# The smallest experts' tiles of a routed layer: 64 rows with high and low parts side by side, two products in place of three

## The chip, the cores and the metric

One core of a Trainium2 chip. The metric is the time of one execution on the device in microseconds; the kernel before takes 1523.02 us in the median of three runs.

## What is computed

Three parts, one behind the other (cut to what matters here):

```python
x = attention(q, k, v, proj)           # 2 x 8 heads, 768 tokens, 64 wide; tokens see only keys of their own bucket
x = sinkhorn_moe(x)                    # 8 experts, every token through every expert
def moe2(x, w_skip, w_gate, w1, w2):   # the second layer: 1536 tokens x 512
    do_compute = x @ w_skip > 0
    e_idx = argmax(x @ w_gate, axis=1)             # one expert for each token kept
    for e in range(8):
        h = maximum(x[e_idx == e] @ w1[e], 0)      # 512 -> 1024
        y = gate * (h @ w2[e])                     # 1024 -> 512
    out = x; out[do_compute] += y
```

With the reference's inputs 815 tokens are kept; ordered by their counts in the first 768 tokens, the experts hold 204, 197, 161, 119, 82, 33, 12 and 7 of them.

## The kernel before

Attention, the first layer and the second layer run one behind the other; the change is in the second. There each expert has a slot of 128 or 256 rows. `order()` ranks the experts by their count in the first half of the tokens, and `SLOT` says which slot each rank gets: ranks 0, 1, 2 get slots 0, 2, 4, which hold two tiles of 128 rows, the others slots with one tile. `route` and `scat` write each token's row into a table in memory; tokens that find no room in their slot are worked off by a reserve loop at the end (`tc.If(n > 0)`), whose number of tiles `extras()` counts.

`TILES = [[0, 8], [1], [2, 9], [3], [4, 10], [5], [6], [7]]` gives the tiles of each slot, in the order of work. For a tile, `gather` fetches its 128 rows by an indirect DMA on GpSimd's queue; `xpose` transposes them on PE (`turn`, L912), ScalarE copies the bank as the high part (fp32r, L914) and VectorE subtracts it to get the low part (L915). `up` multiplies with the first weights (L935), ScalarE applies Relu (L944), `hpose` turns the result in two halves (again `turn`), `down` multiplies with the second weights (L954); VectorE scales and adds the input (`y`, L960), and GpSimd's queue scatters the rows to `out`.

Each f32 product is three fp32r products: high x high, high x low, low x high, with moving operands of 512 columns. The weights come as 1 MB loads on SP's queue; `split` makes one set of 128 x 512, high part on ScalarE (L487), low part on VectorE (L488). A set is asked for by `bget`, which first sees to it that the eight sets behind it have been put into the queues. There are 16 sets for an expert, 8 in `up` and 8 in `down`.

The order of the work is that of the program text. Each step s runs `up` of slot s and then `down` of slot s-1; the turns and transposes of neighbours hang into `up` as jobs, one after each set of weights from the second on:

```python
for s in range(NE):
    jobs = posing([t for t in TILES[s - 1] if t]) if s > 0 else []
    if s + 1 < NE:
        jobs += [lambda t=t: xpose(t) for t in TILES[s + 1]]
    up([t for t in TILES[s] if t], bget, jobs)
    if s > 0:
        down(TILES[s - 1], bget, posing(TILES[s]) if s == NE - 1 else ())
```

So a `down` of a single tile and the `up` of the next single tile stand side by side, and that `up` has up to six jobs. Turns and the banks of `down` share the PSUM pool `mpa` with four banks, which are handed out in turn; a bank is free when ScalarE and VectorE have read it. All queues are in order.

In attention, the set-up of the later layers is strewn among the units of work (`next(m)`): small tables on GpSimd (`bi`, `trip`, `padt`) and their casts on VectorE (`brow`, `tokb`). `padt` has its own place in the pool `kp`. In attention GpSimd makes the low parts of the probabilities (`Pq`, L269) and of v (`r` L230, `vt` L232).

Of the kernel before, what the change touches and what calls it, by code (L numbers as in the profile page):

```python
# [7 lines left out]
F32 = mybir.dt.float32  # L8
R = mybir.dt.float32r
F16 = mybir.dt.float16  # L10
BF = mybir.dt.bfloat16
I32 = mybir.dt.int32
AF = mybir.ActivationFunctionType
ALU = mybir.AluOpType
# [4 lines left out]
NE = 8  # L19
NTOK = 1536  # L20
# [4 lines left out]
TILES = [[0, 8], [1], [2, 9], [3], [4, 10], [5], [6], [7]]  # L25
NST = 11

SLOT = (0, 2, 4, 1, 3, 5, 6, 7)

CLOSE = 0  # L30
PADID = 4000
# [369 lines left out]
def moes(nc, tc, ctx, ident, big, xT, P, g):  # L401
    out = g["out"]
    dram = ctx.enter_context(tc.tile_pool(name="dr", bufs=1, space=DRAM))
    kp = ctx.enter_context(tc.tile_pool(name="kp", bufs=1))
    sp = ctx.enter_context(tc.tile_pool(name="sp", bufs=1))
# [9 lines left out]
    def PS():  # L415
        ring.append(ring.pop(0))
        return P[ring[-1]].tile([128, 512], F32, tag="s", name="mp")
# [189 lines left out]
        nc.vector.tensor_copy(out=tokb[:, :, a].rearrange("p (b j) -> p b j", b=2), in_=ti[:, a])  # L607
    nslot = NE * CAP + 128
    table = dram.tile([nslot, 3], I32, name="table")
    padt = kp.tile([128, nslot // 128, 3], I32, name="padt")  # L610
    nc.gpsimd.memset(padt, 0)
    nc.gpsimd.memset(padt[:, :, 1], int(PADID))
    nc.sync.dma_start(out=table.rearrange("(p j) c -> p j c", p=128), in_=padt)
# [89 lines left out]
    scap = kp.tile([128, 8], F32, name="scap")  # L703
    for r, sl_ in enumerate(SLOT):
        nc.gpsimd.memset(scap[:, r:r + 1], float(sl_ * CAP))
    sbase = kp.tile([128, 8], F32, name="sbase")
    dbl = kp.tile([128, 8], F32, name="dbl")
    perm = kp.tile([128, 8], I32, name="perm")

    def order():  # L710

        ps = PS()
        for j in range(6):
            nc.tensor.matmul(ps[:, 0:8], lhsT=onesb, rhs=rt[0, j][1], start=j == 0, stop=j == 5)
        w = sp.tile([128, 3, 8], F32, tag="ow", name="ow", bufs=1)
        q3 = sp.tile([128, 8, 8], F32, tag="oq", name="oq", bufs=1)
        s3 = [128, 8, 8]

        def row(t):
            return t.unsqueeze(1).to_broadcast(s3)  # L720

        def col(t):
            return t.unsqueeze(2).to_broadcast(s3)
        nc.vector.scalar_tensor_tensor(out=w[:, 0], in0=ps[:, 0:8], scalar=8.0, in1=eid, op0=ALU.mult, op1=ALU.subtract)
        nc.vector.tensor_tensor(out=q3, in0=row(w[:, 0]), in1=col(w[:, 0]), op=ALU.is_gt)
        nc.vector.tensor_reduce(out=w[:, 1], in_=q3, axis=AX.X, op=ALU.add)
        nc.vector.tensor_tensor(out=q3, in0=row(eid), in1=col(w[:, 1]), op=ALU.is_equal)
        nc.vector.tensor_tensor(out=q3, in0=q3, in1=row(scap), op=ALU.mult)
        nc.vector.tensor_reduce(out=sbase, in_=q3, axis=AX.X, op=ALU.add)
        nc.vector.tensor_scalar(out=dbl, in0=w[:, 1], scalar1=float(len(DOUBLE)) - 0.5, scalar2=128.0, op0=ALU.is_lt, op1=ALU.mult)  # L730
        nc.vector.tensor_copy(out=ebb, in_=sbase[0:1, :])
        nc.vector.tensor_tensor(out=q3, in0=row(sbase), in1=col(ebase), op=ALU.is_equal)
        nc.vector.tensor_tensor(out=q3, in0=q3, in1=row(eid), op=ALU.mult)
        nc.vector.tensor_reduce(out=w[:, 2], in_=q3, axis=AX.X, op=ALU.add)
        nc.vector.tensor_copy(out=perm, in_=w[:, 2])
# [149 lines left out]
    xgs = {}  # L885
    gt = {}
    hh = {}
    ht = {}
    hf = {}
    dn = {}  # L890

    def bank(name):
        return P[name].tile([128, 512], F32, tag="s", name="mp")

    def rows_of(t):
        return first[:, 0] if t == 0 else ids[:, t]

    def gather(t, at=None):
        if t == 0:
            xg = P["rx"].tile([128, 512], F32, tag="y", name="xg", bufs=2)  # L900
        else:
            xg = P["m2"].tile([128, 512], F32, tag="xg", name="xg", bufs=8)
        nc.gpsimd.indirect_dma_start(out=xg, out_offset=None, in_=out,
                                     in_offset=bass.IndirectOffsetOnAxis(ap=rows_of(t)[:, 0:1] if at is None else at, axis=0),
                                     bounds_check=NTOK - 1, oob_is_err=False)
        xgs[t] = xg

    def turn(src, tag, bufs):

        ps = bank("mpa")  # L910
        for c in range(4):
            nc.tensor.transpose(ps[:, 128 * c:128 * c + 128], src[c], ident)  # L912
        o = P["xo" if tag == "x3" else "m2"].tile([128, 2, 512], R, tag=tag, name=tag, bufs=bufs)
        nc.scalar.copy(out=o[:, 0, :], in_=ps)  # L914
        nc.vector.tensor_tensor(out=o[:, 1, :], in0=ps, in1=o[:, 0, :].bitcast(F32), op=ALU.subtract)  # L915
        return o

    def xpose(t):
        v = xgs[t].rearrange("p (q a) -> p a q", a=4)
        gt[t] = turn([v[:, c, :] for c in range(4)], *(("xt", 3) if t else ("x3", 1)))  # L920

    def hpose(t, q):
        v = hh[t].rearrange("p (q a) -> p a q", a=8)
        ht.setdefault(t, []).append(turn([v[:, 4 * q + c, :] for c in range(4)], "hT", 4))

    def up(tiles, nget, jobs=()):
        jobs = list(jobs)
        for t in tiles:
            hf[t] = [bank("mpb"), bank("mpb")]
        for k in range(8):  # L930
            w = nget()
            c, h_ = divmod(k, 2)
            for t in tiles:
                for n, (a, i_) in enumerate(((0, 0), (0, 1), (1, 0))):
                    nc.tensor.matmul(hf[t][h_], lhsT=gt[t][:, a, 128 * c:128 * c + 128], rhs=w[:, i_, :],  # L935
                                     start=c == 0 and n == 0, stop=c == 3 and n == 2)
            if k > 0 and jobs:
                jobs.pop(0)()
        for f in jobs:
            f()  # L940
        for t in tiles:
            hh[t] = P["m2"].tile([128, 1024], F32, tag="hf", name="hf", bufs=2)
            for h_ in range(2):
                nc.scalar.activation(out=hh[t][:, 512 * h_:512 * h_ + 512], in_=hf[t][h_], func=AF.Relu)  # L944

    def down(tiles, nget, jobs=()):
        jobs = list(jobs)
        for t in tiles:
            dn[t] = bank("mpa")
        for c in range(8):  # L950
            w = nget()
            for t in tiles:
                for n, (a, i_) in enumerate(((0, 0), (0, 1), (1, 0))):
                    nc.tensor.matmul(dn[t], lhsT=ht[t][c // 4][:, a, 128 * (c % 4):128 * (c % 4) + 128], rhs=w[:, i_, :],  # L954
                                     start=c == 0 and n == 0, stop=c == 7 and n == 2)
            if c > 2 and jobs:
                jobs.pop(0)()
        for t in tiles:
            y = P["rx"].tile([128, 512], F32, tag="y", name="y", bufs=2)
            nc.vector.scalar_tensor_tensor(out=y, in0=dn[t], scalar=rows_of(t)[:, 2:3].bitcast(F32), in1=xgs[t], op0=ALU.mult, op1=ALU.add)  # L960
            nc.gpsimd.indirect_dma_start(out=out, out_offset=bass.IndirectOffsetOnAxis(ap=rows_of(t)[:, 1:2], axis=0),
                                         in_=y, in_offset=None, bounds_check=NTOK - 1, oob_is_err=False)


    XB = {}
# [60 lines left out]
    for b in range(2):  # L1026
        accs[b] = big.tile([128, 6, 512], F32, tag="big", name="acc")
        acc = accs[b]
        for e in range(NE):
            last = b == 1 and e == NE - 1  # L1030
            hs = []
            for fc in range(4):
                w = W1.pop(fc)
# [20 lines left out]
                p = prod(0, 0)  # L1054
# [15 lines left out]
                p = prod(5, 6)  # L1070
# [13 lines left out]
                p = prod(2, 3)  # L1084
# [3 lines left out]
                for h_, c_ in ((h0, ca), (h1, cb)):  # L1088
                    nc.vector.scalar_tensor_tensor(out=h_[:, 1, :], in0=c_.rearrange("p a t -> p (a t)"), scalar=0.0,  # L1089
                                                   in1=h_[:, 0, :].bitcast(F32), op0=ALU.max, op1=ALU.subtract)  # L1090
# [4 lines left out]
            if last:  # L1095
# [6 lines left out]
                for t in range(6):  # L1102
                    y = PS()
                    for i in range(8):
# [5 lines left out]
                        n = 8 * (t - 4) + i  # L1110
# [20 lines left out]
                        for n, (a, i_) in enumerate(((0, 0), (0, 1), (1, 0))):  # L1131
                            nc.tensor.matmul(y, lhsT=hs[i][:, a, 128 * t:128 * t + 128], rhs=W2[i][:, i_, :],  # L1132
                                             start=i == 0 and n == 0, stop=i == 7 and n == 2)
                    nc.vector.scalar_tensor_tensor(out=acc[:, t, :], in0=y, scalar=Pm[:, 6 + t, e:e + 1], in1=acc[:, t, :],
                                                   op0=ALU.mult, op1=ALU.add)
# [16 lines left out]
            for i in range(8):  # L1152
                hook()
                w = W2.pop(i)
                h = hs[i]
                for t in range(6):
                    for n, (a, i_) in enumerate(((0, 0), (0, 1), (1, 0))):
                        nc.tensor.matmul(ys[t], lhsT=h[:, a, 128 * t:128 * t + 128], rhs=w[:, i_, :],  # L1158
                                         start=i == 0 and n == 0, stop=i == 7 and n == 2)
# [9 lines left out]
            for t in range(6):  # L1169
                y = ys[t]  # L1170
                p = Pm[:, 6 * b + t, e:e + 1]
# [25 lines left out]
    nc.vector.tensor_tensor(out=ab, in0=listp[:, 0:2], in1=ab, op=ALU.add)  # L1197
    nc.vector.scalar_tensor_tensor(out=second, in0=ab[:, 0:1], scalar=16.0, in1=ab[:, 1:2], op0=ALU.mult, op1=ALU.add)
    gather(8, second)
    load_rest()  # L1200
    hpose(0, 1)
    tg = [t for tiles in TILES for t in tiles if t not in (0, 8)]
    for t in tg[:7]:
        gather(t)
    tg = tg[7:]
    xpose(8)

    def posing(tiles):
# [18 lines left out]
    n = nc.values_load(xidx["n"][0:1, 0:1], min_val=0, max_val=NXT)  # L1227
    with tc.If(n > 0):
        for x in range(NXT):
            t = NST + x  # L1230
# [3 lines left out]
            def nget():  # L1234
                kind, h_, i = own.pop(0)
                if i == 0:
                    cur["r"] = load_raw(kind, t, h_, "raw")
                return split(cur["r"][:, 512 * i:512 * i + 512], nc.vector)
# [54 lines left out]
```

## Time and profile before

| | |
|---|---|
| median of 3 runs | 1523.02 us (1520.9 to 1524.86) |
| profiled execution | 1523.56 us, span 1521.7 us |
| PE busy | 1415.9 us, 93% |
| PE weight loads busy | 1240.7 us, 82% |
| VectorE busy | 899.5 us, 59% |
| ScalarE busy | 653.8 us, 43% |
| GpSimd busy | 895.9 us, 59% |
| chain that ended last | PE 59%, DVE 19%, POOL 15%, issue 3% |

The second layer lies between about 1364 and 1521.7 us. Shares over the whole span say little about it: its stages are read one by one below. In the rows, PE is TensorE's products and PEld its weight loads, DVE is VectorE, ACT ScalarE, POOL GpSimd. An instruction's time in a row reaches to its end, while the next may start before: VectorE's instructions on 128 x 512 show about 0.68 us each and follow each other every 0.60 us.

### The profile page before, as it was taken

How to read it: one execution, taken by the hardware profiler on the slowest of the kernel's cores; microseconds unless marked ns; L12 is line 12 of the kernel's file. 1: busy time of each engine (PE TensorE's matmuls, PEld its weight loads, DVE VectorE, ACT ScalarE, POOL GpSimd, SP SyncE). 2: the span in 40 equal slices, each digit the busy share in tenths (PEclk: the TensorE clock that was granted, in tenths of full speed). 3: DMA queues.
4: the chain of work that ended last, by engine and by line, in shares of the span. 5: the costliest groups of instructions: out<-in, count | busy, mean ns of one | idle time of the engine just before them, and what ended most of it. 6: DMA issues, size and time to landing. Idle time of an engine off the chain costs nothing.

```text
span 1521.7 us, 21039 instructions
## 1 busy us (share of the span) xinstructions
PE 1415.9 (93%) x7747; PEld 1240.7 (82%) x7747; DVE 899.5 (59%) x1778; ACT 653.8 (43%) x1015; POOL 895.9 (59%) x763
## 2 busy tenths in 40 slices
PE   6788777799999999999999999999999999998997
PEld 5677666578889889899898888989899898876886
DVE  7899989977625336254264736426244262555876
ACT  4777767742423333233333433333133232325665
POOL 3666666764665767657677656856667565512111
PEclk7999999999999999999999999999999999999999
DMA  5999999902121121211211412121211212527762
GB/s 148 192 207 202 203 200 183 171 30 82 57 83 56 56 83 57 83 56 56 84 56 56 164 58 56 56 83 56 83 56 56 84 56 84 194 67 241 258 249 69
DMA packets 224224, 166.27 MB, mean 109 GB/s; under 512 B 160023, under 2 KB 199063, under 8 KB 219761
## 3 DMA queue, kind: packets, MB, share of 16 engines
q1 hardware_dynamic: 219520, 154.69, 38.2%
q10 hardware_dynamic: 2448, 5.58, 1.7%
q0 software_dynamic: 2144, 4.57, 0.9%
q8 instruction: 63, 1.03, 0.3%
q14 instruction: 49, 0.39, 0.1%
HBM read 113.04 MB, written 7.77 MB: 79 GB/s over the span
## 4 chain that ended last, share of the span: by engine, by line
PE 59%; DVE 19%; POOL 15%; issue 3%; ACT 2%; DMA 1%; ACTq 0%; POOLq 0%; DVEq 0%
PE mp L1158 30%; PE mp L1041 15%; POOL w L473 8%; DVE m L252 5%; PE mp L935 4%; PE mp L954 4%; DVE m L254 3%; PE mp L1132 2%; DVE X L298 2%; POOL w L488 2%; POOL T L465 1%; DVE r L296 1%; POOL T L464 1%; DVE t L184 1%; PE mp L912 1%
## 5 line engine op out<-in xcount | busy, mean ns | idle before, releaser
L1158 PE MATMUL mp<-w,h 128*128 128x512 f32 x2160 | 501.5, 393 | 0.0
L1041 PE MATMUL mp<-x,w 128*128 128x384 f32 x2688 | 479.9, 337 | 14.5 <-POOL w L473 9.3
L1041 PEld LDWEIGHTS mp<-x,w 128*128 128x128 f32 x2688 | 467.2, 188 | 22.9 <-POOL w L473 14.1
L1158 PEld LDWEIGHTS mp<-w,h 128*128 128x128 f32 x2160 | 404.5, 188 | 85.8
L488 POOL TENSOR_TENSOR w<-raw,w 128x512 fp32r<-128x512 f32 x127 | 177.4, 1397 | 235.3 <-ACT w L487 235.3
L487 ACT CAST w<-raw 128x512 fp32r<-128x512 f32 x256 | 151.2, 620 | 193.3 <-PE mp L1158 175.1
L1175 DVE SCALAR_TENSOR_TENSOR acc<-mp,Pm,acc 128x512 f32<-128x512 f32 x78 | 54.1, 749 | 291.9 <-PE mp L1158 291.9
L269 POOL TENSOR_TENSOR Pq<-P,Pq 128x768 f16<-128x768 f32 x96 | 158.2, 1653 | 94.7 <-ACT Pq L266 87.0
L473 POOL TENSOR_TENSOR w<-raw,w 128x512 fp32r<-128x512 f32 x124 | 128.9, 1060 | 95.5 <-ACT w L469 95.5
L1085 ACT ACTIVATE h<-ca 128x768 fp32r<-128x768 f32 x64 | 54.3, 848 | 235.4 <-DVE ca L1049 235.4
L473 POOL TENSOR_TENSOR w<-T,w 128x1024 fp32r<-128x1024 f32 x62 | 149.7, 2415 | 0.0
L471 ACT CAST w<-T 128x1024 fp32r<-128x1024 f32 x64 | 67.3, 1052 | 174.2 <-POOL T L466 170.4
L243 PE MATMUL s<-k,t 128*128 128x384 f32 x264 | 70.4, 393 | 37.0 <-ACT P L261 31.7
L284 PE MATMUL b<-vt,T 128*128 128x193 bf16 x576 | 98.8, 261 | 2.5 <-DMA T<-Pq 2.5
L1049 DVE TENSOR_TENSOR u<-mp,p 128x384 f32<-128x384 f32 x64 | 35.6, 556 | 103.2 <-ACT p L1056 61.0
L285 PE MATMUL b<-vt,T 128*128 128x129 bf16 x576 | 95.1, 229 | 0.0
L488 DVE TENSOR_TENSOR w<-raw,w 128x512 fp32r<-128x512 f32 x129 | 84.3, 696 | 12.7 <-ACT w L487 12.5
L261 ACT ACTIVATE P<-s,m 128x768 f32<-128x768 f32 x66 | 65.4, 991 | 55.0 <-DVE m L254 35.1
L243 PEld LDWEIGHTS s<-k,t 128*128 128x128 f32 x264 | 48.7, 211 | 46.4 <-ACT P L261 38.8
L266 ACT CAST Pq<-P 128x768 f16<-128x768 f32 x96 | 79.9, 832 | 6.2 <-DMA T<-Pq 3.8
L1089 DVE SCALAR_TENSOR_TENSOR h<-ca,h 128x768 fp32r<-128x768 f32 x64 | 66.5, 1039 | 19.3 <-ACT h L1085 19.3
L1049 DVE TENSOR_TENSOR u<-mp,u 128x384 f32<-128x384 f32 x128 | 66.7, 553 | 18.6 <-PE mp L1041 14.1
(268 smaller groups left out, 1924.5 us busy)
## 6 DMA issues: line engine op xcount, KB each, us to landing
raw<-in_moe_w_dram SPq DMA_DIRECT2D x128, 256.0 KB
raw<-in_moe_w_dram SPq DMA_DIRECT2D x64, 512.0 KB
raw<-in_moe_w_dram SPq DMA_DIRECT2D x32, 1024.0 KB
k<-in_k_dram SPq DMA_DIRECT2D x16, 192.0 KB
q<-in_q_dram SPq DMA_DIRECT2D x16, 192.0 KB
v<-in_v_dram SPq DMA_DIRECT2D x8, 384.0 KB
out_dram<-acc SPq DMA_DIRECT2D x2, 1536.0 KB
k<-k ACTq DMA_DIRECT2D x14, 192.0 KB
```

Of the source, the lines that this page charges most:

```text
L243: nc.tensor.matmul(ps[:, hf, 0:384], lhsT=a[s][h][:, js], rhs=b[s][h][:, 384 * hf:384 * hf + 384], start=n == 0, stop=n == 1)
L252: nc.vector.tensor_reduce(out=m[:, 0, c], in_=w2(ps), axis=AX.XY, op=ALU.min)
L266: nc.scalar.copy(out=PT[u][:, 0], in_=PP[u])
L269: nc.gpsimd.tensor_tensor(out=PT[u][:, 1], in0=PP.pop(u), in1=PT[u][:, 0], op=ALU.subtract)
L284: nc.tensor.matmul(o, lhsT=t[:, n, :], rhs=vt[:, h, ORDER[n], :], start=n == 0, stop=False)
L285: nc.tensor.matmul(o[:, 0:129], lhsT=t[:, 6 + n, :], rhs=vt[:, h, ORDER[n], 0:129], start=False, stop=n == 5)
L473: tl(out=w[:, 1, c0:c1], in0=src, in1=wf[:, 0, c0:c1], op=ALU.subtract)
L487: nc.scalar.copy(out=w[:, 0, :], in_=v)
L488: eng.tensor_tensor(out=w[:, 1, :], in0=v, in1=w[:, 0, :].bitcast(F32), op=ALU.subtract)
L1041: nc.tensor.matmul(dst, lhsT=w[:, i_, 2 * blk + c, :], rhs=x[:, x_, c, :], start=n == 0, stop=n == 5)
L1049: nc.vector.tensor_tensor(out=o, in0=a, in1=b_, op=ALU.add)
L1158: nc.tensor.matmul(ys[t], lhsT=h[:, a, 128 * t:128 * t + 128], rhs=w[:, i_, :], start=i == 0 and n == 0, stop=i == 7 and n == 2)
```

## The change

The three smallest experts (ranks 5, 6, 7) get the slots 1, 3 and 5, whose tiles now hold 64 rows; ranks 3 and 4 get slots 6 and 7. In such a tile the stationary block of 128 columns holds 64 columns of high parts and 64 of low parts, so that two products, with the weights' high and low part, give the whole: the upper 64 rows of the result belong to the high part, the lower 64 to the low part. `hpose` adds the two halves while it transposes, by a product with `fold`, two identities of 64 stacked; Relu moves from `up` into the eviction of that product. After `down`, ScalarE moves one half and VectorE adds it. `dbl` takes 64 from the room of the small slots. `padt` moves into a buffer of the pool `sp`, tag `x2t`, that `bi` used before it.

```diff
+SMALL = (1, 3, 5)
-SLOT = (0, 2, 4, 1, 3, 5, 6, 7)
+SLOT = (0, 2, 4, 6, 7, 1, 3, 5)
...
-    padt = kp.tile([128, nslot // 128, 3], I32, name="padt")
+    padt = sp.tile([128, nslot // 128, 3], I32, tag="x2t", name="padt", bufs=2)
+    fold = kp.tile([128, 64], F32, name="fold")
+    nc.vector.tensor_tensor(out=fold, in0=ident[:, 0:64], in1=ident[:, 64:128], op=ALU.add)
...
+        nc.vector.tensor_scalar(out=w[:, 2], in0=w[:, 1], scalar1=float(NE - len(SMALL)) - 0.5, scalar2=-64.0, op0=ALU.is_gt, op1=ALU.mult)
+        nc.vector.tensor_tensor(out=dbl, in0=dbl, in1=w[:, 2], op=ALU.add)
...
+    def pairs(o, a):
+        return o[:, 0].rearrange("p (c a t) -> p c a t", c=4, a=2)[:, :, a]
+
+    def turn64(mm, tag, bufs, relu):
+
+        ps = bank("mpa")
+        for c in range(4):
+            mm(c, ps[:, 64 * c:64 * c + 64])
+        pv = ps[:, 0:256].rearrange("p (c t) -> p c t", c=4)
+        o = P["m2"].tile([128, 2, 512], R, tag=tag, name=tag, bufs=bufs)
+        if relu:
+            nc.scalar.activation(out=pairs(o, 0), in_=pv, func=AF.Relu)
+            nc.vector.scalar_tensor_tensor(out=pairs(o, 1), in0=pv, scalar=0.0, in1=pairs(o, 0).bitcast(F32),
+                                           op0=ALU.max, op1=ALU.subtract)
+        else:
+            nc.scalar.copy(out=pairs(o, 0), in_=pv)
+            nc.vector.tensor_tensor(out=pairs(o, 1), in0=pv, in1=pairs(o, 0).bitcast(F32), op=ALU.subtract)
+        return o
+
+    def terms(t):
+
+        return ((0, 0), (0, 1)) if t in SMALL else ((0, 0), (0, 1), (1, 0))
...
     def xpose(t):
         v = xgs[t].rearrange("p (q a) -> p a q", a=4)
+        if t in SMALL:
+            gt[t] = turn64(lambda c, o: nc.tensor.transpose(o, v[0:64, c, :], ident[0:64, 0:64]), "xt", 3, False)
+            return
...
     def hpose(t, q):
         v = hh[t].rearrange("p (q a) -> p a q", a=8)
-        ht.setdefault(t, []).append(turn([v[:, 4 * q + c, :] for c in range(4)], "hT", 4))
+        if t in SMALL:
+            o = turn64(lambda c, o: nc.tensor.matmul(o, lhsT=v[:, 4 * q + c, :], rhs=fold, start=True, stop=True), "hT", 4, True)
+        else:
+            o = turn([v[:, 4 * q + c, :] for c in range(4)], "hT", 4)
+        ht.setdefault(t, []).append(o)
...
-                for n, (a, i_) in enumerate(((0, 0), (0, 1), (1, 0))):
+                for n, (a, i_) in enumerate(terms(t)):
...
             y = P["rx"].tile([128, 512], F32, tag="y", name="y", bufs=2)
...
+            m, d = (64, y) if t in SMALL else (128, dn[t])
+            if t in SMALL:
+                nc.scalar.copy(out=y[0:64], in_=dn[t][64:128])
+                nc.vector.tensor_tensor(out=y[0:64], in0=dn[t][0:64], in1=y[0:64], op=ALU.add)
+            nc.vector.scalar_tensor_tensor(out=y[0:m], in0=d[0:m], scalar=rows_of(t)[0:m, 2:3].bitcast(F32), in1=xgs[t][0:m],
+                                           op0=ALU.mult, op1=ALU.add)
```

The change also moves instructions. On PE, at the end of `up([2, 9])`, then `down([1])` (the row with `hT`) and the start of `up([3])` with the first two turns (`hf`), before:

```order
L912 MATMUL mp<-ident,xg 128x128 x4
L935 MATMUL mp<-w,xt 128x512 x24
L954 MATMUL mp<-w,hT 128x512 x24
L935 MATMUL mp<-w,xt 128x512 x6
L912 MATMUL mp<-ident,hf 128x128 x4
L935 MATMUL mp<-w,xt 128x512 x3
L912 MATMUL mp<-ident,hf 128x128 x4
```

and now:

```order
L951 MATMUL mp<-ident,xg 128x64 x4
L972 MATMUL mp<-w,xt 128x512 x24
L991 MATMUL mp<-w,hT 128x512 x16
L972 MATMUL mp<-w,xt 128x512 x4
L919 MATMUL mp<-ident,hf 128x128 x4
L972 MATMUL mp<-w,xt 128x512 x2
L919 MATMUL mp<-ident,hf 128x128 x4
```

Further on in the same `up([3])`, from the fourth turn to the first products of `down([2, 9])`, now, with the waits (the same ones stood there before):

```order
L919 MATMUL mp<-ident,hf 128x128 [waits DVE_49]
L919 MATMUL mp<-ident,hf 128x128 x3
L972 MATMUL mp<-w,xt 128x512 x2
L919 MATMUL mp<-ident,xg 128x128 [waits DMASW2_49,DVE_49]
L919 MATMUL mp<-ident,xg 128x128 x3
L972 MATMUL mp<-w,xt 128x512 x2
L919 MATMUL mp<-ident,xg 128x128 [waits DMASW3_49,DVE_49]
L919 MATMUL mp<-ident,xg 128x128 x3
L972 MATMUL mp<-w,xt 128x512 x2
L991 MATMUL mp<-w,hT 128x512 [waits DVE_49]
L991 MATMUL mp<-w,hT 128x512 x2
L991 MATMUL mp<-w,hT 128x512 [waits DVE_49]
```

Two products stand between two turns, three before; each `xpose` and the first product into each bank of `down` wait for VectorE.

On VectorE, at the end of `down([1])` and the first turns of `up([3])`, now (before, the row `y<-mp,y` was not there, and `y` read the bank):

```order
L490 TENSOR_TENSOR w<-raw,w 128x512 x12
L1000 TENSOR_TENSOR y<-mp,y 64x512
L1001 SCALAR_TENSOR_TENSOR y<-y,ids,xg 64x512
L490 TENSOR_TENSOR w<-raw,w 128x512 x2
L922 TENSOR_TENSOR hT<-mp,hT 128x512
L490 TENSOR_TENSOR w<-raw,w 128x512
L922 TENSOR_TENSOR hT<-mp,hT 128x512
```

One instruction more stands ahead of the two low parts and the turns.

On POOL, in attention, with the waits, now (before, the first memset of `padt` waited for nothing):

```order
L596 IOTA bi 128x128
L603 IOTA trip 128x12 x2
L615 MEMSET padt 128x291 [waits DVE_49]
L616 MEMSET padt 128x97 [waits Pool_49]
L232 TENSOR_TENSOR r_2370<-v,vt 128x768
L271 TENSOR_TENSOR Pq<-P,Pq 128x768 [waits DMAHW0_49,Activation_49]
```

The memset waits for VectorE's reading of `bi`, and `r` and `Pq` stand behind it.

## Rows read from the trace of the kernel before

**Rows 1.** Table by stage: stretch, its length, busy us (instructions) of each engine, clock, DMA.

```profile
1420.40:1434.20 13.80, 13.80 (x74) 11.82 (x73) 12.54 (x22) 12.32 (x25) 2.65 (x2) 1.00 0.93 335
1434.20:1445.20 11.00, 11.00 (x50) 9.02 (x49) 7.40 (x12) 7.14 (x13) 0.18 (x1) 1.00 0.84 292
```

**Rows 2.** Chain of waits, second layer: start us, us, engine, tile, line, count.

```profile
1420.45 5.49 PE mp L954 x24
...
1427.32 0.44 PE mp L912 x4
...
1434.22 10.99 PE mp L954 x48
...
1457.61 5.49 PE mp L954 x24
```

**Rows 3.** Timeline of VectorE: start us, us, instruction, shapes, count, idle before and releaser.

```profile
1421.91 4.91 DVE L488 TENSOR_TENSOR w<-raw,w 128x512 fp32r<-128x512 f32 x8 [1.26 <-ACT w L487]
1426.74 0.74 DVE L960 SCALAR_TENSOR_TENSOR y<-mp,ids,xg 128x512 f32<-128x512 f32 x1
1427.40 1.28 DVE L488 TENSOR_TENSOR w<-raw,w 128x512 fp32r<-128x512 f32 x2
1428.60 0.68 DVE L915 TENSOR_TENSOR hT<-mp,hT 128x512 fp32r<-128x512 f32 x1
...
1429.80 0.68 DVE L915 TENSOR_TENSOR hT<-mp,hT 128x512 fp32r<-128x512 f32 x1
...
1440.41 0.69 DVE L488 TENSOR_TENSOR w<-raw,w 128x512 fp32r<-128x512 f32 x1 [0.52 <-ACT w L487]
...
1459.07 1.29 DVE L488 TENSOR_TENSOR w<-raw,w 128x512 fp32r<-128x512 f32 x2 [3.21 <-ACT w L487]
```

**Rows 4.** Timeline of PE, the products of the first single `down`.

```profile
1420.29 5.66 PE L954 MATMUL mp<-w,hT 128*128 128x512 f32 x24
```

**Rows 5.** Plain f32 products: a group by shape; rows of the chain, transposes too.

```profile
L672 PE MATMUL mp<-Pm,ones 128*128 128x96 f32 x16 | 3.0, 269 | 1.6 <-DVE Pm L661 1.6
...
360.84 0.19 PE mp L672 x2
...
1341.87 0.43 PE mp L753 x4
...
1352.25 0.79 PE mp L762 x8
```

**Rows 6.** Timeline of ScalarE: ten casts of weights behind the Relu of `up`.

```profile
1421.25 5.31 ACT L487 CAST w<-raw 128x512 fp32r<-128x512 f32 x10
```

**Rows 7.** Waits from 1380 us on: a cast of weights; total us, times, longest.

```profile
ACT w L487 <- DVE w L488: 5.3, 7, 0.8
```

**Rows 8.** Timeline of GpSimd in attention.

```profile
223.70 0.33 POOL L611 MEMSET padt<- 128x291 int32 x1
...
224.24 1.61 POOL L230 TENSOR_TENSOR r<-v,vt 128x768 f32<-128x768 f32 x1
225.81 1.64 POOL L269 TENSOR_TENSOR Pq<-P,Pq 128x768 f16<-128x768 f32 x1
```

**Rows 9.** Timeline of VectorE in attention.

```profile
223.49 0.15 DVE L254 SCALAR_TENSOR_TENSOR m<-m 128x1 f32<-128x1 f32 x1
...
224.61 1.26 DVE L254 SCALAR_TENSOR_TENSOR m<-m 128x1 f32<-128x1 f32 x1
...
226.51 1.09 DVE L298 TENSOR_TENSOR X<-r,m 128x128 f32<-128x128 f32 x1
...
227.65 0.21 DVE L596 CAST brow<-bi 128x128 bf16<-128x128 int32 x1
...
229.26 0.55 DVE L231 CAST vt<-r 128x768 bf16<-128x768 f32 x1
```

**Rows 10.** Chain of waits, attention: shares by line, and one row of L298.

```profile
by line: DVE m L252 28.5%; DVE m L254 18.6%; DVE X L298 10.1%; DVE r L296 7.3%; DVE t L184 5.3%; DVE m L253 4.9%; DVE k L184 4.4%; issue 4.2%; DVE sg L211 2.8%; DMA T<-Pq 2.4%; PE s L199 1.5%; POOL Pq L269 1.5%; DVE m L297 1.5%; DVE m L295 
...
237.30 0.29 DVE X L298
```

More of the change, by code (lines that the diff above doesn't have):

```diff
@@ L902, in gather @@
             xg = P["m2"].tile([128, 512], F32, tag="xg", name="xg", bufs=8)
-        nc.gpsimd.indirect_dma_start(out=xg, out_offset=None, in_=out,
-                                     in_offset=bass.IndirectOffsetOnAxis(ap=rows_of(t)[:, 0:1] if at is None else at, axis=0),
+        n = 64 if t in SMALL else 128
+        nc.gpsimd.indirect_dma_start(out=xg[0:n], out_offset=None, in_=out,
+                                     in_offset=bass.IndirectOffsetOnAxis(ap=rows_of(t)[0:n, 0:1] if at is None else at, axis=0),
                                      bounds_check=NTOK - 1, oob_is_err=False)
@@ L933, in up @@
             for t in tiles:
-                for n, (a, i_) in enumerate(((0, 0), (0, 1), (1, 0))):
+                for n, (a, i_) in enumerate(terms(t)):
                     nc.tensor.matmul(hf[t][h_], lhsT=gt[t][:, a, 128 * c:128 * c + 128], rhs=w[:, i_, :],
-                                     start=c == 0 and n == 0, stop=c == 3 and n == 2)
+                                     start=c == 0 and n == 0, stop=c == 3 and n == len(terms(t)) - 1)
             if k > 0 and jobs:
@@ L943, in up @@
             for h_ in range(2):
-                nc.scalar.activation(out=hh[t][:, 512 * h_:512 * h_ + 512], in_=hf[t][h_], func=AF.Relu)
+                nc.scalar.activation(out=hh[t][:, 512 * h_:512 * h_ + 512], in_=hf[t][h_], func=AF.Copy if t in SMALL else AF.Relu)
     def down(tiles, nget, jobs=()):
@@ L952, in down @@
             for t in tiles:
-                for n, (a, i_) in enumerate(((0, 0), (0, 1), (1, 0))):
+                for n, (a, i_) in enumerate(terms(t)):
                     nc.tensor.matmul(dn[t], lhsT=ht[t][c // 4][:, a, 128 * (c % 4):128 * (c % 4) + 128], rhs=w[:, i_, :],
-                                     start=c == 0 and n == 0, stop=c == 7 and n == 2)
+                                     start=c == 0 and n == 0, stop=c == 7 and n == len(terms(t)) - 1)
             if c > 2 and jobs:
@@ L959, in down @@
             y = P["rx"].tile([128, 512], F32, tag="y", name="y", bufs=2)
-            nc.vector.scalar_tensor_tensor(out=y, in0=dn[t], scalar=rows_of(t)[:, 2:3].bitcast(F32), in1=xgs[t], op0=ALU.mult, op1=ALU.add)
-            nc.gpsimd.indirect_dma_start(out=out, out_offset=bass.IndirectOffsetOnAxis(ap=rows_of(t)[:, 1:2], axis=0),
-                                         in_=y, in_offset=None, bounds_check=NTOK - 1, oob_is_err=False)
+            m, d = (64, y) if t in SMALL else (128, dn[t])
[4 more added lines that the diff above has]
+                                           op0=ALU.mult, op1=ALU.add)
+            nc.gpsimd.indirect_dma_start(out=out, out_offset=bass.IndirectOffsetOnAxis(ap=rows_of(t)[0:m, 1:2], axis=0),
+                                         in_=y[0:m], in_offset=None, bounds_check=NTOK - 1, oob_is_err=False)
     XB = {}
```

## The prediction

> **What bounds the kernel now.** I read the table by stage of the second layer first, then the chain of waits inside it, then the queues of VectorE and ScalarE in the stretches that get shorter, and last GpSimd's queue in attention, because the change touches it too.
>
> In the table [rows 1], PE is busy for the whole of the stretches (13.80 of 13.80 us, 11.00 of 11.00), at the full granted clock (1.00); VectorE is busy for 12.54 and 7.40 us of them. So what is taken off PE there comes off the time, as long as no one else becomes late. The chain [rows 2] runs on PE alone: 24 products of `down` for a single tile take 5.49 us, 48 take 10.99 us, so one product costs 0.229 us, and the four transposes of a turn cost 0.44 us.
>
> The stretch to watch is `down([1])` followed by `up([3])` with six turns hung into it (1420.3 to 1434.2), and its like at `down([3])`, `up([5])` with five. VectorE's rows [rows 3] run without a gap there: eight low parts of weights (L488) from 1421.91, the output row `y` (L960) at 1426.74, two more low parts, then turn and low part in alternation, one of each per 1.20 us, from 1428.60. With T the first product of `down([1])`, 1420.29 [rows 4], VectorE starts its first low part at T+1.62 and its first turn at T+8.31. The second stretch repeats it: from its row in the chain to the first low part are 1.46 us in both (1420.45 to 1421.91, 1457.61 to 1459.07). PE needs 3 products and a turn, 1.13 us, for each of these 1.20. The two are nearly even now, and the change shortens PE's side alone.
>
> **The change, part by part.**
>
> *Fewer products.* Tiles 1, 3 and 5 take two products where they took three: 8 fewer in `up` and 8 fewer in `down`, 16 for a tile, 48 in all. 48 x 0.229 = **11.0 us** off PE. The stationary block has 128 columns before and after, so I take the same 0.229 for one of the new products.
>
> *The turn that adds halves.* `hpose` of a small tile becomes four plain f32 products with the 64-column `fold` in place of four transposes. The kernel before has no such product with 64 columns, but two near it: L762 with 9 columns and L672 with 96. Each call of theirs shows as two records (16 for the 8 of L672, 8 for the 4 of an L762 row), and in the chain eight records of L762 take 0.79 us and two of L672 0.19 us [rows 5]: 0.099 and 0.095 us for one, whatever the columns. 64 lies between 9 and 96, so a turn is 8 x 0.098 = 0.79 us, 0.35 more than 0.44; six of them cost **+2.1 us** (ends: 0.76, for six +1.9; 0.88, if a record cost what one of the four transposes does, 0.11, for six +2.6). All six hang in `up` of full tiles and of tile 6, where PE sets the pace, so they count in full. That a call shows as two records is what I go by; four are among the rivals.
>
> *Transposes of the gathered rows* (three `xpose`, 64 columns for 128): the cheapest four transposes in the chain cost 0.43 us [rows 5], and the weight loads stay; 0.
>
> *Smaller evictions.* The nine turns of small tiles move 256 columns in place of 512 on ScalarE and VectorE. They stand in stretches where VectorE waits for PE anyway (at 1440.41 it has idled 0.52 us before a low part [rows 3]); 0.
>
> *The output of a small tile.* ScalarE copies half of the bank, VectorE adds (one instruction more, 0.60 us by the spacing of its low parts and turns), then the old `y`. Nobody waits for the output itself: it is scattered far from the end, and the last tile, 7, is a full one. But the addition stands in VectorE's queue between the eight low parts and the turns, and so everything behind it is 0.60 us later. ScalarE's copy waits for the end of `down`, with two casts of weights behind it; ScalarE's ten casts took 5.31 us from T+0.96 [rows 6], so the copy comes at T+5.1, after PE's end at T+3.7, and delays nothing that VectorE has not delayed more.
>
> *What is late next.* PE's side of the stretch is now 16 products, 3.66 us; 4 products to the first turn, at T+4.58; then a turn and 2 products, 0.90 us each, so it would start its first `xpose` at T+8.2. VectorE starts its turns at T+8.91, 10.11, 11.31 and 12.51 and frees their banks 0.68 later: T+9.59, 10.79, 11.99, 13.19. PSUM pool `mpa` has four banks, handed out in turn: the fifth of these takes the first turn's bank, and the listed waits say the same (the piece of the order with `[waits ... DVE_49]`). So PE waits at the first `xpose` from 8.2 to 9.59, **1.4**; at the second from 10.5 to 10.79, **0.3**; at the first bank of `down([2,9])` from 11.7 to 11.99, **0.3**; at its second bank, three products on, from 12.68 to 13.19, **0.5**: 2.5 us. In the second stretch there is one `xpose`: 1.4 there, then 0.4 at the second bank of `down([4,10])`: 1.8 us. In `up([7])`, three products and two turns, PE reaches `down([6])` at T+10.1, after the turns; 0. `up([1])` has no small `down` ahead of it; 0. Together **+4.3 us**, bounds 0 (the banks are free when wanted) and 6.0 (VectorE 0.4 us later at each of the four turns).
>
> *Weights.* The loads are as many and as large. In the waits of this layer no cast of weights waits for a DMA, only for VectorE [rows 7] or PE; with VectorE the slower, loads are not wanted faster than now: 0.
>
> *GpSimd in attention.* `padt` moves into a buffer of tag `x2t` that held `bi`, so its memset now waits for VectorE's cast `brow` (see the order of POOL). Before, the memset ran at 223.70 and `brow` at 227.65 [rows 8, 9]. Behind the memset on GpSimd stand `r` and the low part `Pq`; VectorE's cast `vt` waits for `r`. If `brow` stayed at 227.65, `r` would end at 230.05 instead of 225.85, and VectorE, which is the chain in attention, would stand 0.8 us before `vt` at 229.26. But two VectorE instructions there are long only while GpSimd works: L254 took 1.26 us, up to the end of `r`, and 0.15 at 223.49; L298 took 1.09 us beside `Pq`, and 0.29 at 237.30 [rows 9, 10]. With GpSimd halted, they would be 1.1 and 0.8 us shorter and `brow` earlier by as much, and part of it would be lost again when `r` runs later. I take **0**, bounds -1.1 and +0.8. `fold` itself and two small instructions in `order` are under 0.2 us each; the latter stand beside PE's products.
>
> **Sum.** -11.0 + 2.1 + 4.3 + 0 = -4.6 us. Against the profiled execution (span 1521.7, 1523.56 us in all) 1519.0; the median of the runs shown is 0.54 us under that execution, so against the median 1523.02 the forecast is **1518.4 us**. That is 0.30% faster, on the very line: 0.3% (4.6 us) is about what a measurement of this kernel can tell from no change.
>
> **The rivals.**
> - *PE does not wait for banks*: -8.9 us, 1514.1. It needs VectorE's turns 1.4 us earlier than its rows before plus one addition; for it, that the other three waits are small and hang on the first. Against it, that VectorE has no gap from T+1.62 to the turns.
> - *GpSimd's wait lands on the path*: the whole 4.2 us from 223.70 to 227.9 is handed on through `Pq`, its transpose and exp; -0.4 us, 1522.6. For it, that GpSimd's queue is in order and three `P` buffers are all; against it, that the chain there names VectorE's lines and hardly GpSimd's [rows 10].
> - *A product with `fold` takes four records, not two*: a turn is 16 x 0.098 = 1.57 us, 0.78 more than in the sum, six of them 4.7 us; 1523.1. Against it, that both rows of plain f32 products show two for a call [rows 5]. [...]
> - *A small slot overflows* (slower): tokens past 64 of the three smallest experts go to the reserve loop at the end, one tile of 24 + 24 products with its own loads. Its price from rows: 4 MB at the 292 GB/s of a busy stretch, 14.4 us [rows 1], and the 24 products of `down`, 5.5 us, behind the last load: 20 us or more, 1538. It decides at the 65th token. Against it: the reference's inputs put 33, 12 and 7 tokens on those experts.
>
> **How the numbers follow.** The forecast case has 0.62; its own range is 1516.4 to 1520.4 (the turns' ends, the attention term, two us of run to run), half of it on either side of 0.3%: 0.31 faster, 0.31 same. No bank waits 0.13 (faster); GpSimd's wait 0.12 and four records 0.03 (same); overflow 0.03 (slower); 0.07 for what I do not see (0.02, 0.03, 0.02). Faster 0.46, same 0.49, slower 0.05. The range leaves out the rival without waits, the overflow and a part of the unseen: 1515.0 to 1523.0.
>
> **What would show it.** In the profile after: 48 fewer records of products in the second layer; `fold` turns of 0.79 us in the chain; idle time of PE before the transposes of `xg` in `up([3])` and `up([5])`, ended by VectorE, of about 1.4 us, and smaller ones before the first products of the next `down`; none elsewhere in the layer. On GpSimd a gap before `padt` of 2 to 4 us. Wrong would be: PE without a gap there, a gap in other stretches, `fold` turns over 1 us, or a reserve loop that runs.

## The result and the profile after

The changed kernel takes **1539.93 us** (median of 6 runs, 1537.83 to 1542.29) against 1523.68 before (6 runs, 1520.90 to 1525.45): ratio 1.0111, 95% interval 1.0094 to 1.0127. It is slower by 16 us, where 1518.4 and a range of 1515.0 to 1523.0 were forecast.

Cut into stages by the products on PE (first layer: first to last start of a 512-column product, L1158, now L1200; second layer: first to last start of the products of `up` and `down`), the two profiled executions compare so, in us:

| | to the first layer | first layer | between | second layer | last product to end | span |
|---|---|---|---|---|---|---|
| before | 352.08 | 932.06 | 80.14 | 147.90 | 9.53 | 1521.7 |
| after | 351.04 | 943.74 | 80.44 | 154.11 | 11.24 | 1540.6 |
| difference | -1.04 | **+11.68** | +0.30 | **+6.21** | +1.71 | +18.9 |

Most of the loss lies in the first layer, where neither a line nor the order of an instruction was changed. The products there, by line (count, then shortest/median/longest in ns, first and last start in us), and a stretch of the chain of waits. Before:

```profile
L1158 PE MATMUL mp<-w,h x2160: 387/392/503, 352.1 to 1284.1; 128*128 128x512 f32 x197
```

```profile
559.99 15.11 PE mp L1158 x66
```

After:

```profile
L1200 PE MATMUL mp<-w,h x2160: 390/397/496, 351.0 to 1294.8; 128*128 128x512 f32 x197
```

```profile
560.00 15.23 PE mp L1200 x65
```

In this stretch PE is the chain without a gap in both. 66 products fit in 15.11 us before (0.2289 us each), 65 in 15.23 now (0.2343). The difference of 5.4 ns times 2160 products makes 11.6 of the 11.68 us. The products with 384 columns (L1041, now L1083) start 173 ns apart in both.

In the second layer, rows of the chain that answer to [rows 2] (a single `down`, a turn, the next `down`), with a turn that adds halves (L958) and the transposes of a small tile's rows (L951):

```profile
1422.44 1.73 PE mp L958 x8
...
1428.82 0.62 PE mp L951 x4
...
1435.26 2.82 PE mp L991 x12
...
1448.44 10.81 PE mp L991 x45
```

A fold turn takes 1.73 us where the turn of [rows 2] took 0.44. VectorE in the stretch that answers to [rows 3], after eight low parts from 1436.71 (with T the first product of `down([1])`, now 1435.09):

```profile
1436.71 4.90 DVE L490 TENSOR_TENSOR w<-raw,w 128x512 fp32r<-128x512 f32 x8 [3.81 <-ACT w L489]
1441.53 0.67 DVE L1000 TENSOR_TENSOR y<-mp,y 64x512 f32<-64x512 f32 x1
1442.24 0.74 DVE L1001 SCALAR_TENSOR_TENSOR y<-y,ids,xg 64x512 f32<-64x512 f32 x1
1442.91 1.28 DVE L490 TENSOR_TENSOR w<-raw,w 128x512 fp32r<-128x512 f32 x2
1444.11 0.68 DVE L922 TENSOR_TENSOR hT<-mp,hT 128x512 fp32r<-128x512 f32 x1
```

and PE's waits from 1400 us on (total us, times, longest):

```profile
PE mp L919 <- DVE hT L922: 2.5, 2, 1.2
PE mp L991 <- DVE hT L922: 0.2, 1, 0.2
```

The first turn stands at T+9.02 (forecast T+8.91), and PE waits 1.2 us ahead of the first `xpose` of both stretches (forecast 1.4). Last, the end of GpSimd's queue (start, us, idle before and releaser), before:

```profile
1509.15 0.97 POOL L961 DMA_INDIRECT out_dram<-y,ids  x1 [11.30 <-DVE y L960]
1513.64 0.97 POOL L961 DMA_INDIRECT out_dram<-y,ids  x1 [3.51 <-DVE y L960]
```

and after:

```profile
1528.03 0.97 POOL L1003 DMA_INDIRECT out_dram<-y,ids  x1 [11.56 <-DVE y L1001]
1532.01 0.97 POOL L1003 DMA_INDIRECT out_dram<-y,ids  x1 [3.00 <-DMA out_dram<-y,ids]
```

The last scatter waited for VectorE before; now it waits for the landing of the scatter ahead of it.

### The profile page after: what moved, and what is told of

The parts are those of the page before. It is cut to its first block, busy times and chain, and to the rows that moved or that the text cites. A ratio compares the mean times of both kernels' runs of the same rounds, so it can differ in the third digit from the quotient of the medians.

```text
span 1540.6 us, 20994 instructions
## 1 busy us (share of the span) xinstructions
PE 1431.3 (93%) x7723; PEld 1242.1 (81%) x7723; DVE 902.3 (59%) x1784; ACT 652.1 (42%) x1018; POOL 893.9 (58%) x763
## 4 chain that ended last, share of the span: by engine, by line
PE 55%; DVE 21%; POOL 14%; issue 5%; ACT 2%; DMA 2%; ACTq 0%; POOLq 0%; DVEq 0%
PE mp L1200 30%; PE mp L1083 14%; POOL w L475 8%; DVE m L254 5%; DVE m L256 3%; PE mp L991 3%; PE mp L972 3%; DVE X L300 2%; PE mp L1174 2%; POOL w L490 2%; DVE r L298 1%; POOL T L467 1%; POOL T L466 1%; DVE k L186 1%; DVE t L186 1%
## 5 line engine op out<-in xcount | busy, mean ns | idle before, releaser
L1200 PE MATMUL mp<-w,h 128*128 128x512 f32 x2160 | 512.8, 397 | 0.0
L1083 PE MATMUL mp<-x,w 128*128 128x384 f32 x2688 | 479.7, 337 | 13.5 <-POOL w L475 10.4
L1083 PEld LDWEIGHTS mp<-x,w 128*128 128x128 f32 x2688 | 467.2, 188 | 22.1 <-POOL w L475 15.2
L1200 PEld LDWEIGHTS mp<-w,h 128*128 128x128 f32 x2160 | 405.3, 188 | 96.0
```

The source lines that it names most:

```text
L1083: nc.tensor.matmul(dst, lhsT=w[:, i_, 2 * blk + c, :], rhs=x[:, x_, c, :], start=n == 0, stop=n == 5)
```

## The experiments

**Theory A** says that the loss in the first layer comes from where tiles lie. `padt` (1164 bytes in each partition) left the pool `kp` and `fold` (256 bytes) came, so by the addresses of the built program everything behind it on the left side of SBUF moved down by 928 bytes, `w`, the moving operand of L1200, among it; `h`, its stationary operand, lies on the right side and did not move. **Rival B**: something else that the change does (attention, small tiles, clock, transfers).

### e1: old addresses restored

```diff
-    fold = kp.tile([128, 64], F32, name="fold")
+    fold = kp.tile([128, 296], F32, name="fold")[:, 0:64]
```

> The changed kernel with its fold tile allocated 1184 bytes wide instead of 256 (64 of 296 columns used), so that every tile behind it in SBUF stands at the address it had before the change; nothing else differs. Theory A, the place of tiles: the products of the first layer with 512 moving columns (L1200), whose w moved by 928 bytes against an h that did not move, come back from 234 to 229 ns apart; 2160 of them x 5 ns = 11 us, and 2 us more in the second layer: about 1527 us against 1539.9 of the changed kernel, 0.2% slower than before. Rival B: the first layer is slower for another reason (what the changed attention stage leaves behind, clock, DMA traffic): spacing stays 234 ns and the time 1540.

Measured: 1530.15 us, ratio to before 1.0042 (1.0027 to 1.0058); the first layer takes 934.90 us instead of 943.74, 8.84 less, and the chain shows 0.229 us again:

```profile
559.83 15.34 PE mp L1200 x67
```

The pace is as theory A had it; the total is 3 us above its 1527, with a spread of the 8 runs from 1525.75 to 1533.89.

### e2: the layout alone, without small tiles

```diff
 (kernel before)
-    padt = kp.tile([128, nslot // 128, 3], I32, name="padt")
+    padt = sp.tile([128, nslot // 128, 3], I32, tag="x2t", name="padt", bufs=2)
+    fold = kp.tile([128, 64], F32, name="fold")
+    nc.vector.tensor_tensor(out=fold, in0=ident[:, 0:64], in1=ident[:, 64:128], op=ALU.add)
```

> The kernel before with only padt put into the x2t buffer and the fold tile allocated and filled (not used): no small tiles, slot order as before, but the tiles behind padt 928 bytes lower, as in the changed kernel. Theory A: the 512-column products of the first layer go from 229 to 234 ns; time about 1523.7 - 1 (attention) + 11 + 2.5 = 1536, 0.8% slower than before. Rival B, that small tiles or the slot order slow the first layer: 229 ns and 1522 to 1524.

Measured: 1534.16 us, ratio 1.0081 (1.0064 to 1.0098); first layer 942.67 us, 0.234 us a product (15.23 us for 65). So two thirds and more of the loss come without one small tile. e1 keeps the new attention code, the small tiles and the order of the slots and has the old pace; with both runs B falls for the first layer.

### e3, e7, e8: which address counts

```diff
 e3, e8
-    fold = kp.tile([128, 64], F32, name="fold")
+    fold = kp.tile([128, 280], F32, name="fold")[:, 0:64]
 e7
+    fold = kp.tile([128, 272], F32, name="fold")[:, 0:64]
 e8, ahead of the pool hp
+                    pool(c1, "hpad", bufs=1, side="right")
+                    nc.gpsimd.memset(P["hpad"].tile([128, 8], F32, name="hpad"), 0)
```

> The changed kernel with fold 1120 bytes wide: tiles stand 64 bytes lower than before the change (w at 96 beyond a multiple of 128 bytes instead of 32; the changed kernel has 0). Theory A with the address modulo 64 as what counts: products 229 ns apart as before, 1527 us. Theory A with the address modulo 128, or relative to h (which stands at 96): another spacing, somewhere from 226 to 238 ns. Rival B: 234 ns, 1540.

> The changed kernel with fold 1088 bytes wide: w at 64 beyond a multiple of 128 bytes, h still at 96. So far w at 0, 32, 96 gave 234, 229, 227 ns. If the parity of 32-byte steps decides, 234 as at 0; if the distance to h decides (0 at 96 is best, one step above worst), no worse than 234; the value fills the table.

> The changed kernel with fold 1120 bytes wide (w at 96) and in the first layer a pad of 32 bytes ahead of the pool of h, so that h stands at 64 instead of 96. If the distance between w and h counts (32 here as in the changed kernel, where w is at 0 and h at 96), the first layer's products go back to 234 ns, first layer 13 us longer than with h at 96. If only the place of w counts, they stay at 227 ns. The second layer's hT and xt do not move, and its products stay at 227 to 229 ns in both cases.

Measured: e3 1523.03 us (ratio 1.0007, 0.9995 to 1.0018), e7 1537.74 (1.0101, 1.0081 to 1.0121), e8 1535.96 (1.0089, 1.0071 to 1.0107). The chain in the same stretch, e3:

```profile
559.79 15.41 PE mp L1200 x68
```

e8, where `w` stands as in e3 and only `h` is 32 bytes lower:

```profile
559.94 15.17 PE mp L1202 x65
```

All places tried, in bytes beyond a multiple of 128:

| kernel | w | h | w - h, beyond a multiple of 64 | us a product |
|---|---|---|---|---|
| e3 | 96 | 96 | 0 | 15.41 / 68 = 0.227 |
| before, e1 | 32 | 96 | 0 | 0.229 |
| e7 | 64 | 96 | 32 | 15.40 / 66 = 0.233 |
| e8 | 96 | 64 | 32 | 15.17 / 65 = 0.233 |
| after, e2 | 0 | 96 | 32 | 0.234 |

The place of `w` alone does not decide: 96 is the best value beside `h` at 96 and a bad one beside `h` at 64. What fits these five is whether the two operands lie a multiple of 64 bytes apart. They would also fit a rival: that each operand by itself must stand 32 bytes beyond a multiple of 64. The 24 products of tile 0 in the second layer settle that. Their stationary tile `x3` lies on the left side and moves with `w`, so that both stand at 0 in the changed kernel and at 64 in e7. By their start times in the traces they are 229 and 227 ns apart (medians of 17 spacings in each), while the products with `xt`, at 96 beside the same `w`, are 234 and 232.5 apart. The distance counts, then, and not each place. Within the two groups of the table 1 to 2 ns remain that the distance modulo 64 does not explain. In e8 `hT` and `xt` of the second layer did not move, and its products in `down` stand 227 ns apart, as in e3.

### e4: the stride of the stationary block

The `hf` of a small tile is written permuted, on top of e1, so that `hpose` takes 128 neighbouring columns:

```diff
-        v = hh[t].rearrange("p (q a) -> p a q", a=8)
+        v = hh[t].rearrange("p (a q) -> p a q" if t in SMALL else "p (q a) -> p a q", a=8)
...
+                    nc.scalar.copy(out=hh[t].rearrange("p (a q) -> p q a", a=8)[:, 64 * h_:64 * h_ + 64, :],
+                                   in_=hf[t][h_].rearrange("p (q a) -> p q a", a=8))
```

> As the run with the addresses of before, and in addition the small tiles' hidden rows hf are written permuted by ScalarE's copy, so that the stationary block of a fold product is 128 neighbouring columns instead of every eighth one. Theory C, the stride of the stationary block makes a record of the fold product take 0.216 us where those of L762 (neighbouring columns, 0.099) do not: the turns fall from 1.73 to 0.79 us, six of them 5.6 us, about 1521.5. Rival D, the 64 moving columns or f32 itself cost it: the turns stay at 1.73 us and the time is that of the run without the permutation, give or take 0.5 us for ScalarE's strided copy.

Measured: 1522.09 us, ratio 0.9998 (0.9986 to 1.0010), 8 us under e1, where 5.6 were expected. In the second layer it is 5.93 us (152.49 to 146.56); the rest lies in stages that the edit does not touch. A turn in the chain:

```profile
1408.35 0.84 PE mp L958 x8
```

and the loads of its stationary block, in the changed kernel and in this one (count | busy us, mean ns):

```profile
L958 PEld LDWEIGHTS mp<-fold,hf 128*128 128x128 f32 x48 | 11.9, 332 | 0.3
```

```profile
L958 PEld LDWEIGHTS mp<-fold,hf 128*128 128x128 f32 x48 | 6.3, 191 | 0.5
```

Theory C holds: with every eighth column a load takes 332 ns and a record 0.216 us (1.73 / 8), with neighbouring columns 191 ns and 0.105. The 64 moving columns are the same in both. ScalarE's permuted copies take 1174 ns each instead of some 600; there are six, and no wait of PE for them shows.

### e5, e6: both repairs, and the same layout without small tiles

e5 is e4 with `fold` 280 wide, e6 is e2 with `fold` 280 wide.

> Both repairs together: fold 1120 bytes wide (tiles 64 bytes lower than before the change, where the first layer's 512-column products stood 227 to 228 ns apart) and the small tiles' hidden rows permuted (turns of 0.84 us). If the two effects simply add: 1522.1 of the permuted kernel less what the address gave between the two kernels that differ in it alone (profiled spans 1528.7 and 1522.4, 6.3 us; products alone 2160 x 1.7 ns + second layer 0.5 = 4.2 us): 1516 to 1518. If they do not add (the address gain was a matter of clock and of chance): 1520 or more.

> The kernel before with padt in the x2t buffer and the fold tile (1120 bytes wide, filled, not used), no small tiles: the same addresses as the run with both repairs. What the small tiles are worth at one and the same layout is the difference of the two. Forecast from the recorded sum without the extra price of the turns: 4.6 us, less 1.2 us that the last scatter now waits for the one ahead of it, so this one is 3 to 4 us above the run with both repairs, about 1520. Rival: the small tiles are worth nothing (VectorE is the bound there): both the same.

Measured: e5 1518.76 us, ratio 0.9977 (0.9968 to 0.9986); e6 1517.92, ratio 0.9974 (0.9961 to 0.9986). e5 misses the upper end of its 1516 to 1518 by 0.8 us. Both are faster than both kernels, and the intervals lie on each other: at one and the same layout, and with the cheaper turn, the small tiles are worth nothing that these runs can tell. By stage, e5 against e6: second layer 145.81 against 148.06 us, 2.25 less; from the last product to the end 11.13 against 9.55, 1.58 more. That e6 would be 3 to 4 us above e5 was wrong.

### e9, e10, e11: what holds PE up, and the end

e9 gives GpSimd two of the eight low parts in each `down` of a small tile and the last two; e10 leaves out copy and addition of the halves, so that the small tiles' output lacks the low half of `down`'s product; e11 makes the last three low parts only behind the output of tile 6. All on top of e5:

```diff
 e9, in bproduce
+            e_ = eng or nc.vector
+            if (kind == "b1" and e in (3, 5, 7) and i == 2) or (kind == "b2" and e == 7 and hf == 1 and i > 1):
+                e_ = nc.gpsimd
 e10, in down
-                nc.scalar.copy(out=y[0:64], in_=dn[t][64:128])
-                nc.vector.tensor_tensor(out=y[0:64], in0=dn[t][0:64], in1=y[0:64], op=ALU.add)
...
+            m, d = (64, dn[t]) if t in SMALL else (128, dn[t])
 e11, in bget
-        while bst["set"] <= min(k + 8, len(specs) - 1):
+        while bst["set"] <= min(k + 8, len(specs) - (4 if k < len(specs) - 8 else 1)):
```

> The kernel with both repairs, and GpSimd makes two of the eight low parts of weights that VectorE makes during each down of a small tile (1.46 us each on GpSimd, 0.60 on VectorE) and the last two of the layer. Theory E, PE waits for banks only because VectorE's queue is long there: 1.2 us less on VectorE takes the waits before the first xpose (1.24 us) away in both stretches, and tile 6's output comes 1.2 us earlier, so that the last scatter no longer waits for the one ahead of it: 2.4 + 1.2 = 3.6 us less, about 1515. Rival F, ScalarE (busy 13.25 of 13.30 us in the first stretch) is as late as VectorE: the waits shrink by less than 0.5 us each, and the time stays within 1.5 us of the run with both repairs, 1518.8.

> The kernel with both repairs without ScalarE's copy and VectorE's addition of the two halves of a small tile's output: it leaves out the low-part half of down's product for tiles 1, 3 and 5. Theory E: VectorE's turns come 0.6 us earlier, so the wait ahead of the first xpose falls by 0.6 us in each of the two stretches: 1.2 us less. Theory F: ScalarE loses a copy of 0.59 us, too, so the same or a little more. If neither queue sets the wait, nothing changes.

> The kernel with both repairs, and VectorE takes the output of tile 6 ahead of the last three low parts of weights instead of behind them; nothing else moves. Theory G, the last scatter waits for the landing of the one ahead of it, because small tiles leave VectorE late at the end (from the last product to the end of the span 11.1 us, against 9.5 without small tiles): the scatter of tile 6 goes 1.8 us earlier, from the last product to the end 9.7 us, and the time 1517.4 against 1518.8. Rival: the later low parts make PE wait in down of tile 7 for weights, up to 0.7 us, and less than half of it is left; or the end costs 11.1 us whatever the order.

e9: 1528.22 us, ratio 1.0042 (1.0029 to 1.0054), slower by 9 us than e5. PE's waits show where most of it lies:

```profile
PE mp L973 <- POOL w L490: 5.5, 1, 5.5
PE mp L920 <- DVE hT L923: 1.4, 1, 1.4
PE mp L920 <- DVE y L1005: 0.8, 1, 0.8
```

On GpSimd the low parts stood behind a gather that had waited 13.24 us for VectorE, and started at 1423.97, 5.8 us after `up([3])` (1418.14), which wants them. So this run tells neither E nor F; it shows that GpSimd's queue is no place for work with a due time here.

e10: 1515.24 us, ratio 0.9951 (0.9934 to 0.9968). PE's waits for VectorE's turns in e5, then in e10:

```profile
PE mp L919 <- DVE hT L922: 2.8, 2, 1.4
```

```profile
PE mp L919 <- DVE hT L922: 1.2, 2, 0.6
```

The two waits fall by 1.6 us together, the second layer by 1.70 (145.81 to 144.11): E's 0.6 each, and some more. Whether VectorE or ScalarE sets them stays open, since e10 relieves both: in e5's first such stretch, 1418.29 to 1426.83, 8.54 us long, VectorE is busy for 8.51 and ScalarE for 8.49 of it.

e11: 1520.20 us, ratio 0.9983 (0.9971 to 0.9994), no better than e5. The end of GpSimd's queue:

```profile
1505.80 2.38 POOL L1007 DMA_INDIRECT out_dram<-y,ids  x1 [9.76 <-DVE y L1005]
1512.98 0.97 POOL L1007 DMA_INDIRECT out_dram<-y,ids  x1 [4.80 <-DVEq L1274]
```

Tile 6's output did come earlier (4.27 us ahead of the last one, 2.47 in e5), but its scatter now ran beside the three low parts on VectorE (1505.45 to 1507.32) and took 2.38 us instead of 0.97. The last scatter went out at 1512.98, though its output had been there since 1509.81; the row names VectorE's queue at the program's last branch as the releaser, and when the scatter ahead landed is not on record. PE did not wait more. The end takes 12.30 us. So theory G rests on the rows of the changed kernel and of e5 alone; the longer scatter ate 1.41 us of what was put ahead, and what else held the last one stays open.

## Why the prediction was wrong

*The pace of the products that the change keeps.* "I take the same 0.229" was checked for the stationary block's width only. The failed step is the paragraph on `padt`: its move was weighed as a wait on GpSimd, and nothing was put down for the tiles that lie behind it. The profiled pair shows that price with 11.7 us in the first layer, of which the sum held 0; e2 adds 10.6 there without small tiles, e1 takes 8.8 back, and e8 is 10.6 above e3 (941.69 against 931.12). At one and the same layout the first layer varies by 2 to 3 us from run to run (932.06 before, 934.90 in e1). In the second layer it is 1.6 (154.11 against e1's 152.49; 2.6 between e2 and before).

*Fewer products*: right. At the same layout a single `down` of a small tile takes 3.40 us from first to last start in e5, 5.21 in e6: 1.81 less for 8 products, 0.226 each.

*The turn that adds halves*: mis-sized, 1.73 us instead of 0.79, six times 0.94 = 5.6 us. The number of records was right (8 for a turn), and 0.105 us a record would have been near 0.098, but the rows chosen [rows 5] read neighbouring columns and `hf` is read with a stride of eight. The bounds were taken over the moving columns alone (9 and 96), which tell little here (0.099 and 0.095 us a record, 0.105 with 64 and neighbouring columns); "`fold` turns over 1 us" was named as the sign of a wrong forecast. The rival of four records did not happen, though its 1.57 us lies near the 1.73: L958 shows 48 records in its six turns, two for a product. The missing term is the stride's: the load of a plain f32 product takes 332 ns with it and 191 without. The loads of transposes do not follow the stride so plainly; before, they took 190 ns with every eighth column (`hf`), 205 with every fourth (`xg`) and 140 with neighbouring ones (`acc`):

```profile
L912 PEld LDWEIGHTS mp<-ident,hf 128*128 128x128 f32 x88 | 13.0, 190 | 2.3 <-ACT hf L944 0.5
L912 PEld LDWEIGHTS mp<-ident,xg 128*128 128x128 f32 x44 | 7.1, 205 | 6.5 <-DMA xg<-out_dram,second 5.7
...
L753 PEld LDWEIGHTS mp<-ident,acc 128*128 128x128 f32 x24 | 3.0, 140 | 0.8
```

In the pace only the plain products show the stride of eight (0.216 against 0.105 us a record): four transposes took 0.44 us with it and 0.43 without [rows 2, 5].

*What is late next*: right in place, and in size as a whole. VectorE's first turn came at T+9.02, PE waited 1.2 to 1.4 us ahead of each first `xpose`, and between e6 and e5, with the 1.82 us of the missing products put back, the two `up` lost 1.90 and 1.67 us and the `down` behind each 0.79 and 0.33: 4.7 us (forecast 4.3). The list of waits names 3.0 of it in e5: the two ahead of the first `xpose`, and of the four smaller ones forecast only one, of 0.2 us; the rest is spread over the stretches. PE shows no other wait from 1400 us on, so the weights and the smaller evictions were rightly put at 0.

*Transposes of small tiles*: not 0; 0.62 us for four instead of 0.43, three times 0.19 = 0.6 us.

*The output of a small tile*: "nobody waits for the output itself" looked at the small tiles only. At the end VectorE is later by the work added ahead, tile 6's output comes 2.75 us ahead of the last one instead of 4.48, and the last scatter stands until the one ahead has landed. It starts 1.49 us after its output is there (1530.52), 0.28 before, which is 1.2 of the +1.7 us from the last product to the end; all kernels with small tiles have 10.97 us or more there, both without them (e2, e6) 9.66 or less.

*GpSimd in attention*: the gap ahead of `padt` is there, 2.28 us, inside the 2 to 4 foretold:

```profile
223.58 0.34 POOL L615 MEMSET padt<- 128x291 int32 x1 [2.28 <-DVE brow L598]
```

While GpSimd stood, VectorE's L256 and L300 (L254 and L298 before) took 0.15 and 0.29 us where they had taken 1.26 and 1.09, as the prediction had it. The first layer starts 1.04 us earlier, but among the runs with this same attention code its start lies between 349.50 and 353.91, so a gain or loss of a microsecond is not told.

*Sum.* -4.6 + 11.7 + 1.6 + 5.6 + 0.6 + 1.7 = +16.6 us against +16.3 between the medians. That they meet so closely is in part luck: in the second layer the terms make 3.2 us and the profiled pair shows 6.2. This pair is 18.9 apart in all; of the rest 1.2 us are 21 products at the start of `up([8])` (7.83 us, before 6.58) under a granted clock of 0.53 over 1388 to 1399 us, where before it was 0.53 over 1377 to 1384 only. e6, without small tiles, has the long stretch, too (0.53 over 1366 to 1377). In the pair it lies where PE stands waiting for the gather of rows (5.5 us before, 6.2 after) and just behind that wait; what sets its length is not shown. The rivals missed the sign: the only one that ended slower was the reserve loop, and it did not run. Of the two things that decided, one was not in the list, and the other stood there as a bound too narrow.

## What to carry to other kernels

A tile moved to another pool moves the tiles behind it (here by 928 bytes, and 0.229 us a product became 0.234); before a kernel with new buffers is compared, compare the pace of instructions that nobody touched, and put the addresses back to see what the change itself is worth. Before a duration is borrowed from a row of the same operation, compare how the stationary operand is read: here a stride of eight columns made 0.216 us a record of 0.105. Work taken off PE in a stretch where VectorE and ScalarE are even with it can come back as waits: between e6 and e5, 10.9 us of products left 2.2, since 4.7 came back as waits and 3.3 went into the dearer turns and transposes (the `up` of tiles 2 and 9, of 4 and 10, and of 6 are longer by 1.22, 1.21 and 0.86 us).

## What the runs showed of the hardware

- 512-column products with moving and stationary operand a multiple of 64 bytes apart in a partition started 0.227 and 0.229 us apart, at an odd multiple of 32 bytes 0.233 to 0.234 (five layouts, by the addresses of the built programs). Why is not shown. The products with 384 columns (173 ns before and after) tell nothing about it: both their operands lie on the left side and moved together.
- A stationary block of plain f32 read with a stride of 32 bytes took 332 ns to load (changed kernel), 191 with neighbouring columns (e4), and a record of its product 0.216 against 0.105 us. The load of a transpose took 190 ns with this stride, 205 with one of 16 bytes and 140 with neighbouring columns; four transposes took 0.44 us with the stride of 32 bytes and 0.43 with neighbouring columns.
- GpSimd's scatter took 0.97 us beside an idle VectorE (the last one before and after) and 2.38 beside three low parts (e11). Other scatters of the second layer took from 0.97 us (before, at 1485.80) to 2.02 (after, at 1447.80) beside low parts and turns, so a run beside them does not by itself give the time. What makes the 1.41 us no run here shows.
